# A logarithm and exponential in place of GpSimd's power, with norms, loads and weight conversion placed at other times

## Chip, cores, metric

One core of one Trainium2 chip. The metric is the device time of one execution in microseconds (us), lower is better.

## The reference, cut to what matters

```python
# q, k, v: (8, 12, 448, 64) fp32; weights (768, 1024) and (1024, 768), delivered as fp64
rms = np.sqrt(np.mean(x * x, axis=-1, keepdims=True) + 1e-06)      # for q and for k
q_n, k_n = q / rms_q * g_q, k / rms_k * g_k
attn = softmax(q_n @ k_n.T / 8);  o = attn @ v                     # per batch and head
x = o.transpose(0, 2, 1, 3).reshape(3584, 768)
h = x @ w_in;  solu = h * softmax(h);  ln = layernorm(solu) * g_ln
return ln @ w_out
```

48 head pairs (8 batches of 6) go through attention; 28 token tiles of 128 go through the feed-forward part, a tile as soon as its batch is done. Both are mixed on the same engines. The fp64 weights are taken apart into fp32 on the chip, in 28 conversion steps (12 for `w_in`, 16 for `w_out`).

## The kernel before: the parts that matter

```python
LAG = 5; UB = LAG + 2                       # feed-forward tiles waiting; buffers of tag "u"
loads = tile_pool(bufs=2)                   # q and k of a pair
def load_w(step):
    raw = work.tile([P, n, 2], U32, tag="u", bufs=UB)   # shares its buffers with the waiting tiles
    nc.sync.dma_start(raw, ...)
def convert_w(step, raw):                   # cut: five VectorE (six for w_out), two ScalarE instructions
    # ...
    if dst is w_in: nc.gpsimd.tensor_tensor(dst, m, e, OP.mult)
    else: nc.vector.scalar_tensor_tensor(dst, m, gcol, e, OP.mult, OP.mult)
def norm(n):
    nc.scalar.activation(sq, d["qk"], AF.Square)
    nc.vector.tensor_reduce(flat, sq, AX, OP.add)                    # rs: 112 x 16
    nc.vector.tensor_scalar(rs, rs, 1.0 / D, 1e-6, OP.mult, OP.add)
    nc.gpsimd.tensor_tensor(flat, flat, mhalf, OP.pow)               # 1/rms
    nc.gpsimd.tensor_tensor(d["qn"], d["qk"][:, 0], rs[:, 0], OP.mult)
def scores(n, kc):                          # cut: two matmuls, then
    nc.scalar.activation(E, s, AF.Exp, scale=rs_k)                   # per head
    nc.gpsimd.tensor_tensor(es, ..., E, OP.add)                      # from kc = 1
def pair(n):                                # order of emission
    # kc=0: scores; kc=1: scores, load(n+2), norm(n+1), values(n-1); kc=2: scores; kc=3: scores, qk_transpose(n+1)
W_IN = 9; W_OUT = 19     # conversion spread over these pairs; feed-forward halves not before them
```

The order in which the library's scheduler issues instructions on each engine follows the emission above as a priority, not strictly.

## Time and profile before

| | before |
|---|---|
| time, median | 1151.9 us |
| TensorE (PE) busy | 1048 us, 91% |
| VectorE (DVE) / ScalarE (ACT) / GpSimd (POOL) busy | 499 / 388 / 534 us |
| table loads on ScalarE | 1 |

In the profile, PE is TensorE's matmuls, PEld its weight loads; L numbers are lines of the kernel. A group `E<-s` writes `E` from `s`. `[2.4 <-ACT E]` behind an instruction is the idle time of its engine just before it and what ended it. The tables by stretch give each engine's busy us and, in brackets, its instructions. The lines themselves stand in the prediction below.

### The profile page before, as it was taken

What the parts mean: (1) busy time and instruction counts of PE and PEld (TensorE: products, weight loads), DVE (VectorE), ACT (ScalarE), POOL (GpSimd) and SP (SyncE); (2) the same over time, 40 slices, a digit from 0 to 9 for tenths busy, and PEclk for the clock granted to TensorE, in tenths of its full rate; (3) what the DMA queues carried; (4) which work ended last, traced back from release to release, by engine and by line L of the source; (5) the groups of instructions that cost most, each with busy time, mean ns of one, the idle gap of its engine ahead of it and who ended that gap; (6) DMA issues with size and microseconds to landing.
All of it is one profiled execution on the core that took longest, in us unless ns stands there. A gap on an engine that the chain in (4) does not pass through costs nothing.

```text
span 1151.0 us, 10603 instructions
## 1 busy us (share of the span) xinstructions
PE 1048.1 (91%) x3905; PEld 486.6 (42%) x3905; DVE 499.5 (43%) x778; ACT 388.2 (34%) x677; POOL 534.1 (46%) x289
## 2 busy tenths in 40 slices
PE   3648998697799999999999999999999999999997
PEld 1213333333244444444444444444444444355554
DVE  4787477756854323433332335343332333132200
ACT  4444544434443322322233223522234223211111
POOL 5878965546584434543346434753336433200000
PEclk9877999799889999999999999999999999999999
DMA  6512222111321111111112111311112110000001
GB/s 185 168 34 49 69 81 90 40 52 46 103 55 46 42 34 51 41 38 25 37 46 54 38 39 33 78 38 24 38 46 54 38 39 1 15 14 16 27 27 44
DMA packets 109045, 57.48 MB, mean 50 GB/s; under 512 B 91056, under 2 KB 101816, under 8 KB 108984
## 3 DMA queue, kind: packets, MB, share of 16 engines
q1 hardware_dynamic: 104640, 45.63, 15.1%
q10 hardware_dynamic: 4344, 11.08, 2.4%
q8 instruction: 33, 0.54, 0.2%
q14 instruction: 28, 0.23, 0.1%
HBM read 45.68 MB, written 11.01 MB: 49 GB/s over the span
## 4 chain that ended last, share of the span: by engine, by line
PE 70%; DVE 8%; POOL 8%; issue 5%; ACT 4%; DMA 2%; SPq 1%; ACTq 0%; POOLq 0%
PE po L615 25%; PE h L572 22%; PE s L518 9%; PE o L538 8%; POOL es L526 5%; PE pt L505 2%; PE sm L544 2%; ACT E L522 2%; DMA qk<-in_k_dram 1%; POOL rs L488 1%; PE pu L605 1%; DVE tmp L453 1%; DVE tmp L448 1%; POOL w_in L457 1%; ACT u L584 1%
## 5 line engine op out<-in xcount | busy, mean ns | idle before, releaser
L572 PE MATMUL h<-w_in,xT 128*128 128x512 f32 x672 | 310.3, 609 | 12.3 <-DVE hsum L592 6.5
L526 POOL TENSOR_TENSOR es<-es,E 112x896 f32<-112x896 f32 x96 | 205.1, 2136 | 224.5 <-ACT E L522 217.8
L615 PE MATMUL po<-w_out,uT 128*128 128x384 f32 x896 | 299.9, 490 | 4.9 <-ACT uT L606 4.8
L522 ACT ACTIVATE E<-s,rs 112x448 f32<-112x448 f32 x384 | 217.9, 634 | 249.7 <-PE s L518 249.5
L615 PEld LDWEIGHTS po<-w_out,uT 128*128 128x128 f32 x896 | 166.6, 190 | 130.5 <-issue 12.6
L518 PE MATMUL s<-qkT 64*112 64x448 f32 x768 | 186.6, 592 | 18.5 <-DVE qkT L509 12.4
L488 POOL TENSOR_TENSOR rs<-rs,mhalf 112x16 f32<-112x16 f32 x48 | 142.7, 2972 | 129.5 <-DVE rs L487 128.3
L572 PEld LDWEIGHTS h<-w_in,xT 128*128 128x128 f32 x672 | 125.1, 193 | 163.2 <-issue 152.2
L538 PE MATMUL o<-E,v 112*64 112x448 f32 x768 | 158.2, 549 | 0.0
L526 POOL TENSOR_TENSOR es<-E 112x896 f32<-112x896 f32 x48 | 104.8, 2183 | 38.0 <-ACT E L522 38.0
L518 PEld LDWEIGHTS s<-qkT 64*112 64x112 f32 x768 | 64.1, 181 | 134.1 <-issue 103.6
L486 DVE TENSOR_REDUCE rs<-sq 112x16 f32<-112x1024 f32 x48 | 58.5, 1218 | 127.4 <-ACT sq L483 122.1
L581 DVE TENSOR_REDUCE hmax<-h 128x1 f32<-128x1024 f32 x28 | 34.3, 1224 | 153.4 <-PE h L572 153.4
L548 DVE STREAM_TRANSPOSE r<-sm 128x448 f32<-128x448 f32 x48 | 30.5, 635 | 160.3 <-PE sm L544 160.3
L538 PEld LDWEIGHTS o<-E,v 112*64 112x64 f32 x768 | 51.6, 138 | 100.8 <-issue 87.2
L616 ACT COPY y<-po 128x384 f32<-128x384 f32 x56 | 26.7, 476 | 198.6 <-PE po L615 198.6
L483 ACT ACTIVATE sq<-qk 112x1024 f32<-112x1024 f32 x48 | 50.8, 1059 | 102.4 <-DMA qk<-in_k_dram 100.8
L505 PE MATMUL pt<-ident,qn 112*128 112x112 f32 x192 | 32.1, 295 | 55.8 <-DVE r L548 46.2
L595 POOL TENSOR_TENSOR he<-he,mhalf 128x1 f32<-128x1 f32 x28 | 15.6, 558 | 140.2 <-DVE he L594 140.1
L509 DVE TENSOR_SCALAR qkT<-pt,gcol 128x448 f32<-128x448 f32 x48 | 32.1, 669 | 60.3 <-PE pt L505 60.3
L505 PEld LDWEIGHTS pt<-ident,qn 112*128 112x128 f32 x192 | 21.0, 153 | 87.9 <-DVE r L548 48.0
L596 DVE TENSOR_SCALAR u<-u,mv,he 128x1024 f32<-128x1024 f32 x28 | 42.0, 1499 | 31.3 <-POOL he L595 31.3
(49 smaller groups left out, 686.0 us busy)
## 6 DMA issues: line engine op xcount, KB each, us to landing
qk<-in_q_dram SPq DMA_DIRECT2D x96, 112.0 KB, 2.8
qk<-in_k_dram SPq DMA_DIRECT2D x96, 112.0 KB, 3.0
v<-in_v_dram SPq DMA_DIRECT2D x48, 224.0 KB, 2.6
out_dram<-y ACTq DMA_DIRECT2D x28, 384.0 KB, 2.3
raw<-in_moe_w_in_dram SPq DMA_DIRECT2D x12, 512.0 KB, 5.6
raw<-in_moe_w_out_dram SPq DMA_DIRECT2D x16, 384.0 KB, 4.1
grow<-in_g_q_dram ACTq DMA_DIRECT2D x2, 0.2 KB
grow<-in_g_k_dram ACTq DMA_DIRECT2D x2, 0.2 KB
```

The source lines that it names most:

```text
L483: nc.scalar.activation(sq, d["qk"].rearrange("p s j h d -> p (s j h) d"), AF.Square)
L486: nc.vector.tensor_reduce(flat, sq, AX, OP.add)
L488: nc.gpsimd.tensor_tensor(flat, flat, mhalf[0:SP].to_broadcast([SP, 4 * NJ]), OP.pow)
L505: nc.tensor.transpose(pt[:, j * SP : (j + 1) * SP], src, ident[0:SP, 0:SP])
L518: nc.tensor.matmul(s, d["qkT"][hh, 1, kc * SP : (kc + 1) * SP], d["qkT"][hh, 0, :], start=True, stop=True)
L522: nc.scalar.activation(d["E"][:, kc, h], d["s", h], AF.Exp, scale=d["rs"][:, 1, kc, h : h + 1])
L526: nc.gpsimd.tensor_tensor(d["es"], d["E"][:, 0] if kc == 1 else d["es"], d["E"][:, kc], OP.add)
L538: nc.tensor.matmul(o[h * D : (h + 1) * D, :], d["v"][:, h, kc * D : (kc + 1) * D], d["E"][:, kc, h], start=(kc == 0), stop=(kc == NJ - 1),)
L572: nc.tensor.matmul(d["h"][:, hs], xTs[m][:, c, i * P : (i + 1) * P], w_in[:, c, hs], start=(c == 0), stop=(c == KD - 1))
L581: nc.vector.tensor_reduce(nmax, d["h"], AX, OP.max, negate=True)
L596: nc.vector.tensor_scalar(u, u, mv[:, 0:1], e, OP.subtract, OP.mult)
L615: nc.tensor.matmul(po, d["uT"][:, c], w_out[:, c, hs], start=(c == 0), stop=(c == KF - 1))
```

## The change

Its intent: take the 2.9 us power off GpSimd, take the norm's chain off the path by starting it earlier, and thin out the weight conversion.

```diff
-    LAG = 5
+    LAG = 4
-        d["qk"] = loads.tile([SP, 2, NJ, 2, D], FP32, tag="qk", name="qk")
+        d["qk"] = loads.tile([SP, 2, NJ, 2, D], FP32, tag="qk", name="qk", bufs=3)
-        nc.vector.tensor_scalar(rs, rs, 1.0 / D, 1e-6, OP.mult, OP.add)
-        nc.gpsimd.tensor_tensor(flat, flat, mhalf[0:SP].to_broadcast([SP, 4 * NJ]), OP.pow)
+        nc.scalar.activation(y, flat, AF.Ln, scale=1.0 / D, bias=eps[0:SP])
+        nc.vector.tensor_scalar(x, flat, -0.5 / D, -0.5e-6, OP.mult, OP.add)
+        nc.scalar.activation(y, y, AF.Exp, scale=-0.5)
+        nc.vector.tensor_tensor(x, x, y, OP.mult)
+        nc.vector.tensor_tensor(x, x, y, OP.mult)
+        nc.vector.scalar_tensor_tensor(flat, x, 1.5, y, OP.add, OP.mult)
# pair(n): load(n+2), norm(n+1) at kc == 1   ->   load(n+3) at kc == 0, norm(n+2) at kc == 2
# (cut: allocation of x, y and eps; load(2) and norm(1) before the loop)
-    W_IN = 9
-    W_OUT = 19
+    W_IN = 12
+    W_OUT = 24
```

More of the change, by code (lines that the diff above doesn't have):

```diff
@@ L412, in fast_path @@
     m896 = consts.tile([P, 1], FP32, name="m896")
+    eps = consts.tile([P, 1], FP32, name="eps")
     def setup():
@@ L416, in setup @@
         nc.gpsimd.memset(m896, -896.0)
+        nc.gpsimd.memset(eps, 1e-6)
         nc.gpsimd.memset(ones, 1.0)
@@ L486, in norm @@
         nc.vector.tensor_reduce(flat, sq, AX, OP.add)
-        nc.vector.tensor_scalar(rs, rs, 1.0 / D, 1e-6, OP.mult, OP.add)
-        nc.gpsimd.tensor_tensor(flat, flat, mhalf[0:SP].to_broadcast([SP, 4 * NJ]), OP.pow)
+        x = small.tile([SP, 4 * NJ], FP32, tag="nx", name="nx")
+        y = small.tile([SP, 4 * NJ], FP32, tag="ny", name="ny")
+        nc.scalar.activation(y, flat, AF.Ln, scale=1.0 / D, bias=eps[0:SP])
[4 more added lines that the diff above has]
+        nc.vector.scalar_tensor_tensor(flat, x, 1.5, y, OP.add, OP.mult)
         d["qn"] = work.tile([SP, NJ * 2, D], FP32, tag="qn", name="qn")
@@ L635, in pair @@
             pieces.append(lambda kc=kc: scores(n, kc))
-            if kc == 1 and n + 2 < B * NP:
-                pieces.append(lambda: load(n + 2))
-            if kc == 1 and n + 1 < B * NP:
-                pieces.append(lambda: norm(n + 1))
+            if kc == 0 and n + 3 < B * NP:
+                pieces.append(lambda: load(n + 3))
+            if kc == 2 and n + 2 < B * NP:
+                pieces.append(lambda: norm(n + 2))
             if kc == 1 and n:
@@ L650, in fast_path @@
     qk_transpose(0)
+    load(2)
+    norm(1)
     wq = [(moe_w_in, w_in, c, slice(i * 512, i * 512 + 512)) for c in range(KD) for i in range(2)]
-    W_IN = 9
-    W_OUT = 19
+    W_IN = 12
+    W_OUT = 24
     n_in = len(wq)
```

## The prediction

> **What bounds the kernel now.** I read the page first: busy shares, then the 40 slices, then the chain that ended last; after that, TensorE by stretch, and last the order of instructions in two stretches of the slow part.
>
> ```profile
> PE 1048.1 (91%) x3905; PEld 486.6 (42%) x3905; DVE 499.5 (43%) x778; ACT 388.2 (34%) x677; POOL 534.1 (46%) x289
> PE   3648998697799999999999999999999999999997
> DVE  4787477756854323433332335343332333132200
> POOL 5878965546584434543346434753336433200000
> PEclk9877999799889999999999999999999999999999
> ```
>
> The average (TensorE 91%) hides two stages. From slice 13 on, about 345 us, TensorE has 9 in nearly every slice: it is the bound there, and VectorE (DVE) and GpSimd (POOL) are at 3 to 5. Before that TensorE has holes, its granted clock sags to 7, and DVE and POOL run at 5 to 8. The windows view in four stretches gives the size (columns: length, busy us of PE, PEld, DVE, ACT, POOL, clock, DMA share, GB/s):
>
> ```profile
> 0.00:111.00 111.00, 61.90 (x235) 26.17 (x237) 80.43 (x108) 50.50 (x85) 82.42 (x51) 0.82 0.39 111
> 111.00:155.00 44.00, 41.23 (x198) 16.13 (x194) 21.59 (x31) 24.36 (x41) 42.64 (x21) 1.00 0.29 72
> 155.00:345.00 190.00, 159.04 (x600) 66.05 (x598) 130.51 (x215) 82.01 (x144) 111.42 (x58) 0.92 0.24 66
> 345.00:1151.00 806.00, 785.95 (x2883) 378.24 (x2878) 266.98 (x425) 231.38 (x408) 297.58 (x160) 1.00 0.13 37
> ```
>
> Now the TensorE floor, from undisturbed stretches of the chain. One attention pair: 16 score matmuls 3.4 us (1.69 per 8), 16 value matmuls 3.16, sums and transposes 1.9 after overlap: 8.4 us. One feed-forward tile: 10.3 (in) + 10.6 (out) + 1.1 (transposes) = 22.0; the tiles at the end of the chain do follow each other at 22.0 us. 48 x 8.4 + 28 x 22.0 = 1019 us. The span is 1151, so **132 us are lost**. Matmul counts by line place them: before 345 us there are 312 of the 768 score matmuls (19.5 pairs), 154 of 672 of feed-forward in (6.4 tiles) and half a tile of feed-forward out, 164 + 66 + 5 = 235 us of TensorE work; so 110 us are lost before 345 us, 22 after.
>
> What holds the first part? POOL's timeline in a plain stretch, and DVE against POOL while weights are converted:
>
> ```profile
> 121.60 2.10 POOL L526 TENSOR_TENSOR es<-E 112x896 f32<-112x896 f32 x1
> 123.81 2.91 POOL L488 TENSOR_TENSOR rs<-rs,mhalf 112x16 f32<-112x16 f32 x1
> 126.80 1.04 POOL L491 TENSOR_TENSOR qn<-qk,rs 112x512 f32<-112x512 f32 x1
> 127.80 4.27 POOL L526 TENSOR_TENSOR es<-es,E 112x896 f32<-112x896 f32 x2
> 132.02 2.08 POOL L526 TENSOR_TENSOR es<-E 112x896 f32<-112x896 f32 x1
> ...
> 39.67 2.07 POOL L526 TENSOR_TENSOR es<-E 112x896 f32<-112x896 f32 x1
> 39.75 2.27 DVE L448 TENSOR_SCALAR tmp<-raw 128x512 uint32<-128x512 uint32 x1 [2.35 <-POOL w_in L457]
> 53.34 0.43 DVE L448 TENSOR_SCALAR tmp<-raw 128x512 uint32<-128x512 uint32 x1 [1.16 <-POOL w_in L457]
> ```
>
> POOL has no gap from 121.6 to 132.0: the pair's period of 10.4 us is POOL's own sum, with the power (L488) 2.91 of it. The two L448 lines are the same instruction, 0.43 us alone and 2.27 us when it starts beside an L526: it ends when POOL ends. So in the conversion stage DVE and POOL largely take turns.
>
> **What the Trainium skill says.** (1) "SBUF — State Buffer", section "Who interferes with whom": a DVE instruction in a 2-port mode, or with two SBUF inputs against a GpSimd instruction that reads SBUF, and a GpSimd instruction exclude each other for the whole instruction. The L448 pair above agrees, and the power once took 4.91 us. (2) "ScalarE: Activation LUTs", section "What ACT_TABLE_LOAD costs": 1283 ns plus about 1380 ns of drain for each change of set; small activations with a pointer bias cost 280 ns plus 0.833 per element. The trace has one load, 1.28 us, and 634 ns for 448 elements (653 by the page). (3) Same page, "Table sets: the hidden batching unit": one set holds both exp and ln, but the usual exp set does not list ln. This trace can't say which set the compiled program will take. (4) "TensorE: Matmul & The Clock Gate", Part 1: an idle array is clocked down; the PEclk row agrees, and so filling the holes also speeds the matmuls. No page prices the power; the trace's 2.9 us stands.
>
> **The change part by part.**
> - POOL loses 48 x 2.97 = 143 us. Per pair it falls from 6.46 (three sums) + 1.04 (qn) + 2.97 = 10.5 to 7.5 us, below the 8.4 of TensorE. Where TensorE is the bound this earns nothing by itself.
> - ACT gains two small activations, estimated 0.29 + 0.20 us from the page, so 6.1 + 0.5 = 6.6 a pair (8 exponentials 4.54, square 1.06, copy 0.54); with 1.1 to 1.3 for a conversion step, 7.9.
> - DVE gains three small instructions (one becomes four), 0.17 us each free (L487) and 0.35 with blocking (L594, the same kind, has a mean of 0.349 against 0.12 free): about 1.1 a pair, 4.7 to 5.8.
> - The latency from reduce to qn falls from about 3.4 (0.17 + 2.91 + hops) to about 1.5, but a norm two pairs ahead and a third load buffer take that chain, and the wait of squares for loads, off the path anyway.
> - Conversion: 12 steps over 12 pairs, then 16 over 12, instead of 9 and 10. Steps done earlier than asked may remain so; their work is unchanged.
> - Feed-forward: counting four pieces a pair, the old order leaves pairs 30, 35, 36, 42 and 47 with none (10 us pairs, as near 730 us), the new order fills every pair from 24 to 47. The tail is 34 pieces against 35. But pairs 15 to 23 now have none. Depth 4 frees the tile for the loads; raw weights share the six remaining buffers with five waiting tiles, so one is left, as before.
>
> **The sum.** In the first stage I take POOL and the DVE instructions that exclude it as one resource, at their free durations. Before, to 345 us: 19.5 x 10.2 (POOL pair) + 12 x 1.26 (w_in) + 3 = 217, conversions 28 x 2.7 = 76, others 9: 302 of 345, or 88%. TensorE by contrast had 235 of 345. After, to the start of pair 24: 24 x 7.3 + 18 = 193, conversions 76, small ones and others 20: 289 us. At the same 88% that is 328 us, by which TensorE has done 24 x 8.4 + 5 x 10.3 = 253. There remain 1019 - 253 = 766, plus 18 lost (22, less a little for the filled pairs): 328 + 784 = 1112. I choose **1115 us**, 3% faster.
>
> **Rivals.**
> - Table loads: if the program goes exp set, ln set, exp set for every pair, that is 96 loads, 123 us of ACT, and per early pair 7.9 + 2.6 = 10.5 us (13 with drains), which puts ACT where POOL was. For it: ln isn't among the usual exp set's functions. Against: the joint set exists. Result 1135 to 1160.
> - The first 12 pairs stay as slow as before (20 us a pair in 0 to 111), because the turns of DVE and POOL and not the power hold them; conversion steps may also still bunch early (all 12 of w_in came by 97 us, half the allotted pairs). Then only some 15 us come back there: 1130.
> - Lost filler: attention pairs without feed-forward expose each wait. At 111 to 155 us the old kernel lost only 3 us because feed-forward in filled in. Nine such pairs at 10.4 instead of 8.4 cost 18 us, up to 1130.
> - Everything hides: the first stage falls to TensorE's own rate at 85%, 298 us to pair 24, and 1080.
>
> **Range and chances.** The best case is 1080; joined rivals give 1150. I give table loads about even odds, and the best case a fifth. Range 1077 to 1152; faster by over 2% (under 1129) 0.60, same 0.32, slower 0.08.
>
> **What would show it right or wrong.** L488 gone, POOL near 390 us busy; the pair period in a plain early stretch 8.5 to 9.5 us with TensorE or DVE rather than POOL ending the waits; PEclk less sagging before slice 13; pair 24 reached near 330 us; no ten-us pairs after it. Busy TensorE stays near 1030. If ACT shows many table loads and waits of exponentials behind them, the first rival holds. The prediction falls if pair 24 comes later than 370 us, or if TensorE gets new holes after it.

## More of the kernel before

Medians are of 3 to 7 runs.

One more is wanted later, the first line of the chain that ended last: shares of the span by engine. Kernel before:

```profile
PE 70%; DVE 8%; POOL 8%; issue 5%; ACT 4%; DMA 2%; SPq 1%; ACTq 0%; POOLq 0%
```

So 8% of the path runs over POOL and 12% over DVE and ACT.

## The result, and the profile after

**1184.06 us** (1183.37 to 1185.17, 4 runs) against 1151.84 (1150.6 to 1152.11, 4 runs) of the kernel before beside it: ratio 1.0283, 95% interval 1.0265 to 1.0301, slower. A ratio here and below is the mean time of one kernel's fast runs over that of the other's of the same rounds, so it is not quite the ratio of the medians.

The page of the changed kernel, in the order of the prediction's lines: busy time, then the span in 40 slices (tenths busy; PEclk the granted clock), the chain's shares by engine, and two groups (count, busy us, mean ns):

```profile
PE 1062.1 (90%) x3905; PEld 483.6 (41%) x3905; DVE 518.3 (44%) x922; ACT 533.1 (45%) x869; POOL 392.5 (33%) x242
PE   3667887997677999999999999999999999999997
DVE  3896445578777344334233434334233433311300
ACT  6666786347776654434343435433343423110111
POOL 2756656144555532223232322223232322200000
PEclk9687999999977999999999999999999999999999
PE 68%; DVE 11%; ACT 11%; DMA 4%; issue 2%; SPq 2%; POOL 1%; ACTq 0%; DVEq 0%; POOLq 0%
L492 ACT ACT_TABLE_LOAD x48 | 61.6, 1283 | 4.6 <-DVE gcol L423 3.8
L494 ACT ACT_TABLE_LOAD x43 | 55.2, 1283 | 0.8
```

POOL lost 142 us, as reckoned, and nearly vanished from the path (8% to 1%). ACT gained 145 us and went from 4% to 11% of it. Most of that is table loads: 48 before the logarithms (L492), 43 before the small exponentials (L494), 5 before the large ones and 1 at the start, 97 x 1.283 = 124 us. TensorE becomes dense (9 without a break) only from the 14th slice, 384 us; in the kernel before it was from the 12th, 317 us. The same four stretches as before:

```profile
0.00:111.00 111.00, 59.76 (x219) 24.11 (x219) 81.33 (x134) 72.86 (x113) 64.11 (x45) 0.81 0.42 114
111.00:155.00 44.00, 37.35 (x185) 15.06 (x184) 17.11 (x39) 34.87 (x56) 24.73 (x14) 0.98 0.22 55
155.00:345.00 190.00, 153.69 (x608) 61.45 (x606) 125.82 (x225) 115.75 (x190) 89.74 (x52) 0.94 0.26 68
345.00:1182.00 837.00, 811.28 (x2900) 383.03 (x2898) 294.05 (x525) 309.58 (x513) 213.96 (x132) 0.99 0.12 35
```

In the first two stretches TensorE does less than before, although POOL is free for 18 us more in each: what POOL gave up, ACT took (22 and 10 us more). POOL's timeline in plain early pairs (start, duration, instruction; the idle before it in brackets):

```profile
126.22 2.10 POOL L535 TENSOR_TENSOR es<-E 112x896 f32<-112x896 f32 x1 [0.89 <-ACT E L531]
131.51 2.09 POOL L535 TENSOR_TENSOR es<-es,E 112x896 f32<-112x896 f32 x1 [3.19 <-ACT E L531]
133.56 1.04 POOL L500 TENSOR_TENSOR qn<-qk,rs 112x512 f32<-112x512 f32 x1
134.56 2.07 POOL L535 TENSOR_TENSOR es<-es,E 112x896 f32<-112x896 f32 x1
137.54 2.10 POOL L535 TENSOR_TENSOR es<-E 112x896 f32<-112x896 f32 x1 [0.91 <-ACT E L531]
```

The period is 11.3 us, not 8.5 to 9.5, and POOL now waits for ACT's exponentials. ACT over one such period:

```profile
126.11 1.06 ACT L485 ACTIVATE sq<-qk 112x1024 f32<-112x1024 f32 x1
127.19 1.28 ACT L492 ACT_TABLE_LOAD   x1
128.48 0.31 ACT L492 ACTIVATE ny<-rs,eps 112x16 f32<-112x16 f32 x1
128.81 1.28 ACT L494 ACT_TABLE_LOAD   x1
130.10 0.21 ACT L494 ACTIVATE ny<-ny 112x16 f32<-112x16 f32 x1
130.22 2.19 ACT L531 ACTIVATE E<-s,rs 112x448 f32<-112x448 f32 x4
132.29 0.55 ACT L516 COPY qkT<-pt 128x448 f32<-128x448 f32 x1
135.25 2.21 ACT L531 ACTIVATE E<-s,rs 112x448 f32<-112x448 f32 x4 [2.42 <-PE s L527]
```

In these lines the pair's later exponentials (130.22) and the copy of the transposed keys (132.29), which the next pair's scores need, come after both loads. A norm that belongs to the pair after next still takes its place in this queue.

Nor did the norm's data leave the path. Of the chain up to pair 24 the landing of the keys takes 32 us here and 14 in the kernel before, the square (L485) 18 and 2, its sum (L488) 17 and 6.

Pair 24's first sum on POOL, in the kernel before (first fence) and in the changed one (second), tells when the second stage starts:

```profile
468.38 2.08 POOL L526 TENSOR_TENSOR es<-E 112x896 f32<-112x896 f32 x1
```
```profile
400.82 2.10 POOL L535 TENSOR_TENSOR es<-E 112x896 f32<-112x896 f32 x1 [1.36 <-ACT E L531]
```

In the changed kernel pair 24 comes at 401 us; the prediction had 328. From there to the end it takes 1181.6 - 400.8 = 781 us; the prediction had 784. Part of this agreement is luck: 5.75 tiles of feed-forward in had been computed by then, not 5, which is 8 us of TensorE work. The whole miss lies before pair 24. (That the old kernel reaches it at 468 is no loss: it has done more feed-forward by then.)

### The profile page after: what moved, and what is told of

Same layout as the page of the kernel before. It is cut to its first block, busy times and chain, and to the rows that moved or that the text cites. A ratio compares the mean times of both kernels' runs of the same rounds, so it can differ in the third digit from the quotient of the medians.

```text
span 1181.6 us, 10970 instructions
## 1 busy us (share of the span) xinstructions
PE 1062.1 (90%) x3905; PEld 483.6 (41%) x3905; DVE 518.3 (44%) x922; ACT 533.1 (45%) x869; POOL 392.5 (33%) x242
## 4 chain that ended last, share of the span: by engine, by line
PE 68%; DVE 11%; ACT 11%; DMA 4%; issue 2%; SPq 2%; POOL 1%; ACTq 0%; DVEq 0%; POOLq 0%
PE po L624 25%; PE h L581 23%; PE s L527 9%; PE o L547 7%; DMA qk<-in_k_dram 3%; ACT E L531 3%; PE pt L514 2%; ACT L494 2%; PE sm L553 2%; SPq L479 2%; ACT sq L485 2%; DVE rs L488 1%; PE pu L614 1%; ACT L492 1%; DVE tmp L450 1%
## 5 line engine op out<-in xcount | busy, mean ns | idle before, releaser
L531 ACT ACTIVATE E<-s,rs 112x448 f32<-112x448 f32 x384 | 221.7, 633 | 243.6 <-PE s L527 241.1
L527 PE MATMUL s<-qkT 64*112 64x448 f32 x768 | 195.5, 609 | 29.3 <-DVE qkT L518 19.4
L535 POOL TENSOR_TENSOR es<-E 112x896 f32<-112x896 f32 x48 | 101.8, 2122 | 261.6 <-ACT E L531 261.6
L547 PE MATMUL o<-E,v 112*64 112x448 f32 x768 | 161.2, 561 | 0.0
L488 DVE TENSOR_REDUCE rs<-sq 112x16 f32<-112x1024 f32 x48 | 58.4, 1217 | 109.4 <-ACT sq L485 109.0
L485 ACT ACTIVATE sq<-qk 112x1024 f32<-112x1024 f32 x48 | 50.7, 1057 | 79.3 <-DMA qk<-in_k_dram 79.1
L500 POOL TENSOR_TENSOR qn<-qk,rs 112x512 f32<-112x512 f32 x48 | 55.8, 1162 | 85.1 <-PE pt L514 59.7
L492 ACT ACT_TABLE_LOAD x48 | 61.6, 1283 | 4.6 <-DVE gcol L423 3.8
L494 ACT ACT_TABLE_LOAD x43 | 55.2, 1283 | 0.8
L495 DVE TENSOR_TENSOR nx<-nx,ny 112x16 f32<-112x16 f32 x48 | 18.1, 377 | 81.4 <-ACT ny L494 81.4
```

Of the source, the lines that this page charges most:

```text
L485: nc.scalar.activation(sq, d["qk"].rearrange("p s j h d -> p (s j h) d"), AF.Square)
L492: nc.scalar.activation(y, flat, AF.Ln, scale=1.0 / D, bias=eps[0:SP])
L494: nc.scalar.activation(y, y, AF.Exp, scale=-0.5)
L500: nc.gpsimd.tensor_tensor(d["qn"], d["qk"][:, 0].rearrange("p j h d -> p (j h) d"), rs[:, 0].rearrange("p j h -> p (j h) ()").to_broadcast ...
L527: nc.tensor.matmul(s, d["qkT"][hh, 1, kc * SP : (kc + 1) * SP], d["qkT"][hh, 0, :], start=True, stop=True)
L531: nc.scalar.activation(d["E"][:, kc, h], d["s", h], AF.Exp, scale=d["rs"][:, 1, kc, h : h + 1])
```

## The experiments

**Lost time by stretch.** All are judged with one number besides the time: the length of a stretch less the TensorE work done in it, at the floors of the prediction (8.4 us a pair, 10.3 a tile in, 11.7 a tile out with its transposes), counted from the matmuls of each line. A matmul across a border counts in both stretches, so an entry can be 1 to 3 us low. In us, of the profiled runs:

| kernel | time | ratio to before | 0-110 | 110-250 | 250-400 | 400-end |
|---|---|---|---|---|---|---|
| before | 1151.8 | 1 | 60 | 24 | 25 | 22 |
| changed | 1184.1 | 1.0283 | 65 | 22 | 47 | 27 |
| e1 changed, one table load | 1159.8 | 1.0058 | 60 | 8 | 43 | 22 |
| e2 changed, with the power | 1158.1 | 1.0042 | 62 | 14 | 35 | 26 |
| e3 before, new 1/rms | 1165.4 | 1.0102 | 61 | 33 | 19 | 30 |
| e4 before, new 1/rms, one load | 1141.8 | 0.9908 | 56 | 19 | 16 | 26 |
| e5 e1, old spread | 1150.1 | 0.9996 | 60 | 19 | 21 | 23 |
| e7 e4, new spread | 1153.6 | 1.0025 | 54 | 10 | 42 | 24 |
| e8 e4, depth 4 | 1145.8 | 0.9958 | 56 | 21 | 22 | 24 |
| e6b e1, raw buffers of its own | 1156.9 | 1.0060 | 60 | 41 | 11 | 22 |
| e9 e4, raw buffers of its own | 1148.1 | 0.9979 | 60 | 35 | 10 | 23 |
| e10 e4, no `w_in` conversion (wrong result) | 1112.5 | 0.9663 | 33 | 21 | 14 | 23 |
| e11 e1, no `w_out` conversion (wrong result) | 1125.8 | 0.9790 | 54 | 9 | 17 | 22 |
| e12 e4, no `w_out` conversion (wrong result) | 1117.2 | 0.9713 | 52 | 11 | 8 | 23 |

The 95% intervals of the ratios are 0.0016 to 0.0029 to either side; at a threshold of 2% the changed kernel counts as slower, e10 and e12 as faster, e11 as unclear and all others as the same. e1 to e4 ran on one chip together, then e5, e7 and e8, then e6b, e9 and e10, then e11 and e12, each with the kernel before. So rows of different groups are compared by their ratios, 0.01 being 11.5 us.

**e1: the table loads alone.** One explicit load at the start of the program, of the set that has both functions (number 6 in the library's list):

```diff
+    nc.scalar.add_instruction(
+        InstLoadActFuncSet(name=..., engine=Activation, act_func_set_id=6))
     with TileContext(nc) as tc:
```

The compiler then places no other load, and in the two traces all other instructions start in the same order on every engine. The result is correct.

> The changed kernel with one table load at the program's start, of the set that holds exp and ln, in place of the 97 loads that the compiler placed; the order of all other instructions is the same. Theory T (the table loads sit in ScalarE's queue on the path of the attention pairs): the early pair period falls from 11.3 to below 9.5 us, and the time from 1184 to 1110-1145 us. Theory R (one raw-weight buffer and the late second half hold pairs 13 to 24; the loads lie beside other waits): within 15 us of 1184.

Measured 1159.8 us: by the ratios 26 us better than the change and 7 us above the kernel before. Between theories: the loads cost, but only about a fifth of the 123 us of loads that left the queue. ACT in the same early pairs:

```profile
123.83 0.55 ACT L516 COPY qkT<-pt 128x448 f32<-128x448 f32 x1
126.80 2.21 ACT L531 ACTIVATE E<-s,rs 112x448 f32<-112x448 f32 x4 [2.42 <-PE s L527]
128.91 1.06 ACT L485 ACTIVATE sq<-qk 112x1024 f32<-112x1024 f32 x1
131.26 0.31 ACT L492 ACTIVATE ny<-rs,eps 112x16 f32<-112x16 f32 x1 [1.29 <-DVE rs L488]
131.60 0.22 ACT L494 ACTIVATE ny<-ny 112x16 f32<-112x16 f32 x1
```

From the square's end to the logarithm's start there are still 1.29 us, now a wait for VectorE's sum: the first load had lain in that wait, and only the second made ACT's sequence longer. Pairs 5 to 12 take (178.4 - 108.5) / 7 = 10.0 us on average instead of 11.3, shorter by one load; so this part of theory T (below 9.5) was too hopeful as well.

**e2: the rest of the change without the new 1/rms.** The power and its `tensor_scalar` restored in the changed kernel.

> The changed kernel with GpSimd's power back, the rest of the change kept. Theory T: no table loads, but the power again on GpSimd: early pairs at about 10.4 us, time near the kernel before, 1140-1165 us. Theory R: the schedule is what costs, so it stays above 1170 us.

Measured 1158.1 us, as theory T had it: without the loads the new schedule is near the kernel before, but 5 us slower by the ratio, not faster. Set beside e1, this run says more: both have the new schedule and one table load, and differ only in how 1/rms is made. Pair 24 in e2 and in e1:

```profile
378.63 2.11 POOL L529 TENSOR_TENSOR es<-E 112x896 f32<-112x896 f32 x1
```
```profile
374.98 2.10 POOL L535 TENSOR_TENSOR es<-E 112x896 f32<-112x896 f32 x1 [1.30 <-ACT E L531]
```

Up to there POOL is busy for 289.5 us in e2 and 211.1 in e1 (VectorE 273.5 and 285.0, ScalarE 209.8 and 223.6). The 78 us less on POOL brought pair 24 forward by 3.6 us, and the whole times are the same within the noise (ratios 1.0042 and 1.0058). POOL's part of the chain up to pair 24 fell from 39 to 8 us, but DMA rose from 28 to 54, VectorE from 112 to 128, ScalarE from 34 to 42.

**e3 and e4: the new 1/rms without the schedule**, e3 as compiled (97 loads), e4 with the one load of e1.

```diff
 # the kernel before; in norm(n) the lines of the change's diff with AF.Ln to OP.add, OP.mult
 # e4 also: the explicit load of e1
```

> The kernel before with the logarithm, exponential and Newton step alone; table loads as the compiler places them. Theory T: slower than before, 1160-1190 us, ScalarE holding early pairs at 11 us or more. Theory R: same or faster than before, 1130-1155 us.

> The kernel before with the logarithm, exponential and Newton step, and one table load of the joint set. Theory T: faster than before, 1115-1140 us, early pair period below 9.5 us. Theory R: the same as e3 within 8 us.

Measured 1165.4 and 1141.8 us, e4 just outside theory T's range. By the ratios the loads cost 22 us here, 26 in the new schedule: the same within the noise. With them the new 1/rms is 1% slower than the power, without them 0.9% faster. POOL in e4, plain early pairs:

```profile
114.49 2.10 POOL L534 TENSOR_TENSOR es<-E 112x896 f32<-112x896 f32 x1 [0.77 <-ACT E L530]
118.40 1.04 POOL L499 TENSOR_TENSOR qn<-qk,rs 112x512 f32<-112x512 f32 x1 [1.81 <-DVE rs L496]
119.40 4.24 POOL L534 TENSOR_TENSOR es<-es,E 112x896 f32<-112x896 f32 x2
124.43 2.10 POOL L534 TENSOR_TENSOR es<-E 112x896 f32<-112x896 f32 x1 [0.78 <-ACT E L530]
```

Without the power POOL has gaps, and the period is 9.9 instead of 10.4 us. So removing 2.9 us from the engine that held this stretch gave 0.5 a pair; its gaps now end with ACT's exponentials and DVE's `rs`. e4 is the fastest correct kernel. What stays open is the other 18 us: e1 and e4 differ in the schedule alone. With the power the same schedule costs only 5 us (e2).

**e5, e7, e8: the schedule taken apart.**

```diff
 # e5: e1 with                     # e7: e4 with                    # e8: e4 with
-    W_IN = 12; W_OUT = 24         -    W_IN = 9;  W_OUT = 19       -    LAG = 5
+    W_IN = 9;  W_OUT = 19         +    W_IN = 12; W_OUT = 24       +    LAG = 4
```

> e1 with the conversion spread over 9 and 19 pairs again; norms two ahead, loads three, depth 4 and the one table load stay. Theory C (the late starts at pairs 12 and 24 cost: pairs 15 to 23 have no feed-forward to fill TensorE): 1125-1143 us, as e4 or faster. Theory B (the norms and loads ahead, or depth 4, cost): stays at 1155-1165 us.

> e4 with only the conversion spread over 12 and 24 pairs. Theory C: slower than e4 by 12 us or more, 1152-1165 us. Theory B: within 6 us of e4.

> e4 with depth 4 and so six shared buffers, nothing else. Theory D (the smaller depth costs filler): slower than e4 by 8 us or more. Otherwise within 5 us of e4.

By ratios: depth 4 alone +0.5% (e8 over e4), then norms and loads ahead +0.4% (e5 over e8), then the new spread +0.6% (e1 over e5); the intervals of the first two steps overlap, so neither is certain. The new spread alone is +1.2% (e7 over e4). The spread is the largest part; its lost time sits in 250 to 400 us (42 and 43 in e7 and e1, 16 to 25 in the kernel before, e3, e4, e5 and e8, which have the old one). The norms and loads ahead gained nothing. e5 fell between its theories: the spread costs, the rest perhaps.

**e6b and e9: is it the raw buffer?** In e1 the raw loads of `w_out` come 7 to 11 us apart between 281 and 341 us, each issued when the step before has read the single free buffer, and raw loads are 16% of the chain from 253 to 375 us. Theory U says that this is what makes pairs 15 to 23 take 13.6 us ((375.0 - 252.8) / 9). A first version, e6, did not build: too little on-chip memory. In e6b the room comes from elsewhere:

```diff
-        raw = work.tile([P, n, 2], U32, tag="u", name="raw", bufs=UB)
+        raw = work.tile([P, n, 2], U32, tag="u" if n == 512 else "raw", name="raw", bufs=UB if n == 512 else 2)
-        d["y"] = work.tile([P, DM], FP32, tag="y", name="y")
+        d["y"] = work.tile([P, DM], FP32, tag="y", name="y", bufs=1)
 # and bufs 4 -> 3 for the small tiles, 2 for x and y of the norm, still 4 for rs
```

> e1 with two buffers of their own for the raw halves of the second weight (room from one out-tile buffer and some small tiles). Theory U (one free raw buffer: the load of each step can only start when the step before has read its buffer, and this load lies on the chain for 16% of 253 to 375 us): the period of pairs 15 to 23 falls from 13.6 to below 12 us, the time by 10 us or more against e1. Theory C (these pairs only lack feed-forward to fill): within 5 us of e1, period above 13 us.

> e4 with the same buffers for the raw halves: a candidate for the best version. Theory U: 4 to 12 us faster than e4 (pairs 15 to 18 wait for raw loads there too), 1130-1138 us. Theory C: as e4, 1139-1144 us.

The stretch from 253 to 375 us, e1 first, then e6b (busy us of PE, PEld, DVE, ACT, POOL, then the clock):

```profile
253.00:375.00 122.00, 92.18 (x416) 35.73 (x414) 92.73 (x167) 67.94 (x132) 69.73 (x38) 0.92 0.33 87
```
```profile
253.00:375.00 122.00, 114.87 (x527) 47.22 (x527) 60.53 (x125) 68.79 (x129) 77.32 (x46) 1.00 0.25 60
```

The mechanism was there: pairs 15 to 23 fall to 9.9 us and TensorE is at 94%. The time does not move (1156.9 us, ratio as e1's), and pair 24 comes at 375.2 us, in e1 at 375.0:

```profile
375.18 2.09 POOL L535 TENSOR_TENSOR es<-E 112x896 f32<-112x896 f32 x1 [0.74 <-ACT E L531]
```

With free buffers the conversion of `w_out` ran earlier (its last instructions at 101 to 183 us, in e1 at 99 to 352), beside pairs 5 to 12, whose period rose from 10.0 to (214.7 - 110.6) / 7 = 14.9 us. The loss moved from one stretch (43 to 11) to the other (8 to 41). So theory U falls as an explanation of the time: the buffer decides where the conversion lies, and here not what it costs. e9 was even slower than e4 by 0.7%; its loss moved in the same way (19 to 35, 16 to 10). What the smaller pools cost in both was not measured apart.

**e10 to e12: what the conversion costs.** For one weight the step is cut to a single ScalarE copy; the result is wrong, the rest of the program stays.

```diff
 def convert_w(step, raw):
+    if dst is w_in:          # e10; w_out in e11 and e12
+        nc.scalar.activation(dst[:, c, cols], hi.bitcast(I32), AF.Copy, scale=2.0 ** -33)
+        return
```

> e4 with a wrong result on purpose: the first weight's conversion is one ScalarE copy a step instead of five VectorE, two ScalarE and one GpSimd instruction. Theory L (VectorE and GpSimd taking turns over the conversion hold the first six pairs at 16 us and more, whatever makes 1/rms): pair 5 is reached by 75 us instead of 103, the time falls by 20 us or more. Otherwise (the attention pairs themselves are slow at the start): pair 5 after 90 us, less than 10 us gained.

Measured 1112.5 us, by the ratios 28 us below e4; pair 5 comes at 77 us instead of 103 (theory L had said 75), and the loss in 0 to 110 us falls from 56 to 33:

```profile
77.18 2.09 POOL L537 TENSOR_TENSOR es<-E 112x896 f32<-112x896 f32 x1 [0.78 <-ACT E L533]
```

So the conversion makes a good part of the slow start, which no version of 1/rms touches: in all other kernels that stretch loses 52 to 65 us. That it does so by VectorE and GpSimd taking turns is not shown apart: the cut takes their work out altogether. The other 33 us stay unexplained.

> e1 with a wrong result on purpose: the second weight's conversion is one ScalarE copy a step instead of six VectorE and two ScalarE instructions. Theory X (in the new schedule this conversion lies in pairs without feed-forward, where nothing fills TensorE, wherever the raw buffers place it): pair 24 is reached 30 us or more earlier than 375 us, the time falls by 25-40 us against e1. Otherwise less than 15 us.

> The same cut in e4, the schedule before. Theory X: the feed-forward beside it hides part of this conversion, so less is gained than in e11, 8-22 us against e4. If as much is gained as in e11 (within 6 us), the schedules don't differ in how much of the conversion they expose, and the 18 us between e1 and e4 have another cause.

Measured 1125.8 and 1117.2 us: by the ratios 31 us gained in the new schedule, 22 in the old. Pair 24 in e11 comes 30 us earlier than in e1:

```profile
344.86 2.10 POOL L538 TENSOR_TENSOR es<-E 112x896 f32<-112x896 f32 x1 [0.70 <-ACT E L534]
```

Theory X holds: the new schedule exposes about 8 us more of the same conversion, half of the 18 us between e1 and e4. The other half remains with this conversion gone (e11 over e12: 1.0079) and has the size of depth 4 plus norms ahead in e8 and e5; its mechanism was not taken further.

## Why the prediction was wrong

Predicted 1115 us, 1077 to 1152, with a chance of 0.08 for a change for the worse of over 2%; measured 1184. Pair 24 came at 401 us, beyond the 370 by which the prediction said it would fall. Point by point:

- **The floor and the two stages: right.** The remainder from pair 24 was put at 784 us; measured 781, and 780 in e1 (with the bit of luck named above). No ten-us pairs came after it. POOL's busy time near 390: 392.5.
- **"POOL loses 143 us ... estimated 0.29 + 0.20 us" for the activations: right** (0.307 and 0.214). Three of the four small VectorE instructions average 0.22 to 0.32 and one 0.38, where half take 0.18 or less: a few last up to 2.05 us and end 0.03 us after a POOL instruction.
- **The first rival, the table loads, was put at even odds and left out of the main sum.** It came true: 97 loads. Its price was over-stated as a path (123 us of ACT) and its result under-stated (1135 to 1160), because it was priced on top of a kernel that would otherwise gain. Measured alone: +22 to +26 us (e4 against e3, e1 against the change).
- **The failed step of the sum is "At the same 88% that is 328 us".** It makes the stage as long as POOL's and VectorE's work together, so that the power's 2.9 us a pair come back in full: 24 x 2.9 / 0.88 = 79 us. Even with the loads gone, pair 24 comes at 375 us (e1), 47 later than the 328; with them at 401. What replacing the power brought to pair 24 was 3.6 us in this schedule (e1 against e2) and 17 in the old one (451.3 in e4 against 468.4), where the same 10 tiles in and 4 out lie before it. By e1 the 289 us of that sum were 77% of the stage. In POOL's place the chain has DMA, VectorE and ScalarE (e2 above), and 30 of the 375 us hang on the conversion of `w_out` (e11). That the 88% came from a stage with 6.9 tiles of feed-forward among the pairs, against 5 here and nine empty pairs, may add to it; that share is not measured apart.
- **"Conversion ... their work is unchanged": true, and the point.** The change moves it to pairs without filler. The third rival, lost filler (18 us, "up to 1130"), saw the place, but counted the 2 us a plain pair lacks and not the conversion that lies there (8 us more exposed than in the old schedule, e11 and e12). Pairs 15 to 23 took 14.3 us in the changed kernel ((400.8 - 272.1) / 9), against the 10.4 of that rival.
- **The second rival, the slow first pairs, held**: pair 5 at 115 us against 111 before. e10 shows the conversion of `w_in` to be a good part of the reason; the turns that the rival named were not tested apart.
- **"Latency ... off the path anyway": wrong.** Loads of keys, square and sum have more of the chain up to pair 24 than before (32, 18 and 17 us against 14, 2 and 6; in e1 22, 9 and 14), and the norm's instructions stand in ScalarE's queue before the exponentials.
- **Smaller signs that failed:** TensorE's busy time rose to 1062 us where it was to stay near 1030, the early period was 11.3 us (10.0 without the loads) and not 8.5 to 9.5, and PEclk still falls to 7 before the dense stage.

The balance, by experiment: new 1/rms without loads -12 us (e4), loads +24 (e3 against e4), schedule +18 (e1 against e4); together +30, of the 32 measured. The parts do not simply add, and the order matters: with the power kept, the schedule alone costs 5 us (e2), and replacing the power after that gains nothing (e1 against e2). So the gain of 12 us exists in the old schedule only; why, was not settled.

## What to carry to other kernels

When ScalarE gets a function that the running set lacks, count the table loads in the compiled program before anything else; if one set serves all, load it once explicitly: here, in the old schedule, a 1% loss became a 1% gain. For work that fills no engine by itself, like this conversion, look for stretches in which the bounding engine has other work queued: spreading it over pairs without such work cost 0.6 to 1.2% here, and buffers of its own only moved its price. (A schedule that puts it wholly beside feed-forward was not tried.) And the sum of two engines' busy times, at an occupancy read from one stage (88%), is no length that shrinks with that sum: take the work away in one run first, as e1 against e2 does, and see what else moves up.

## What the Trainium skill lacked or had wrong

- "ScalarE: Activation LUTs", "What ACT_TABLE_LOAD costs", gives 1283 ns plus about 1380 ns of drain, 2.66 us a switch. Here a load took 1.283 us and the instructions before and after followed within 0.02 us each way (127.19 to 128.48 in the changed kernel): no further drain shows, and a switch cost 1.3 us of the queue.
- The same page, "Table sets: the hidden batching unit", says that ln and exp need one load because a set has both, and its rules for kernel authors say to use that set. That page does not say that the compiled program may not choose it: with functions mixed it placed 97 loads; an explicit load at the start left 1, and the time fell by 22 to 26 us.
- No page prices GpSimd's power: 2.91 us for 112 x 16 elements, against 2.1 us for a sum of 112 x 896.
